# Two heads of q and k share 128 rows in an attention, expert-layer and soft-expert kernel: products and splitting for both heads at once, halves spread by DMA, weight decoding begun two slots later

## The chip, the cores and the metric

One Trainium2 chip, one of its cores. The metric is the device time of one execution in microseconds (us), the median of several runs. The core has five engines with queues of their own: TensorE (PE; its weight loads are listed as PEld), VectorE (DVE), ScalarE (ACT), GpSimd (POOL), and SyncE (SP), which here issues all DMAs.

## The reference, cut to what matters

Three layers run one after the other.

```python
# 1: attention inside clusters; q, k, v are (2, 8, 768, 64), 16 centroids per head
q_assign = argmax(q_n @ c_n.T); k_assign = argmax(k_n @ c_n.T)
mask = q_assign[..., :, None] == k_assign[..., None, :]
scores = where(mask, q @ k.T / sqrt(64), -1e9)
attn = exp(scores - max(scores)); attn /= sum(attn) + 1e-9
x = (attn @ v) laid out as (1536, 512)
# 2: a wide layer with a rational function; w_in and w_out arrive as float64
h = x @ w_in                                   # (1536, 2048)
g = (a0 + a1*h + a2*h**2 + a3*h**3) / (1 + |b0|*|h| + |b1|*h**2 + 1e-6)
x = g @ w_out
# 3: a soft mixture of 8 experts with 4 slots each
logits = x @ phi; slots = softmax(logits, 0).T @ x; each expert: relu(slots @ w1) @ w2
out = softmax(logits, 1) @ expert_outputs
```

## The kernel before

**Slots.** The 16 (batch, head) problems are taken as 8 pairs of heads. A pair has 12 units, one for each of its 2 heads and 6 tiles of 128 query rows, so the attention has 96 slots, numbered `n`; two slots of lead (`LEAD`) come ahead of slot 0. The loop at the end of the attention writes one slot after the other: steps planned for this slot on VectorE and GpSimd (the dictionary `plan`), the transposes of unit n (`turn`, tile `sT`), the exponentials of unit n+1 (`a1_exp`), the copy of `sT` to SBUF (`turned`, tile `eT`), the products of unit n+2 (`a1_mm`, tile `s`), their negated copy with a running minimum on VectorE (`a1_neg`, tile `e`, the row TENSOR_SCALAR_CACHE_REDUCE), planned TensorE steps, and the products with v (`a2_av`, tile `av`). PE, ACT, DVE and POOL keep the order in which the code stands; SP's order is made by a scheduler. `s` and `sT` take turns in two PSUM buffers, so a new `s` waits until the `e` before it has been read, and a new `sT` until the `eT` before it has been copied.

**Preparing a pair.** `prep(p)` returns steps as (offset, kind, function); they are planned four slots into pair p-2 and so spread over the slots behind. They are: products with centroids (`scores`), scaling, transposing (`scT`), argmax (`best`, `first`), a one-hot matrix `oT` and a mask matrix `W`; the part that marks rows of other clusters (`nonhot`, `signed`); and the operands. An fp32 product is made of rounded parts: with a value's rounded high part and the rest as its low part, `q1` holds 64 rows of high and 64 rows of low part, `k1` holds the high part of k twice, and `k2` the low part, with `q2` the high part of q again. A query whose cluster holds no key is zeroed: `alive` is a product that gives 1 or 0 for each query, `qalive` multiplies q by it and by 1/8.

**How the rows lie.** The host hands q and k over transposed and doubled: rows 0 to 63 and rows 64 to 127 of a tile both hold the same head. So a head's split needs no movement between rows: `ksplit(h)` makes `k1` of 128 rows in one GpSimd instruction and `k2` in a second, `qsplit(h, c)` (c is one of two halves of the columns) makes the high part in 128 rows and the low part in rows 64 to 127, and one DMA copies the high rows to `q2`. All of it is done for each head. The first pair has a path of its own (`first_pair`), which runs ahead of the slots. The plan of the second pair's steps is the list `PREP1`.

**Decoding.** Between these steps the float64 weights are turned into fp32, 32 tiles of 128x512 values (`decode_steps`): `bits` (two VectorE instructions), `expo` (ACT), `mant` and `sign` (VectorE), `value` (GpSimd), and for `w_in` `parts` (two on GpSimd), then DMA to DRAM. The list `DEC` says at which slot each tile begins:

```python
DEC = [3 * i if i < 24 else 72 + 2 * (i - 24) for i in range(2 * NF)]
```

**Idle products.** `idle(n)` issues n products of a zero tile, whose result nobody reads. They stand between the steps ahead of the slots and, at the end of the loop's body, in one slot:

```python
        if n < -1:
            idle(2)
```

Behind the attention come 48 units of the wide layer (`h_mm`, `s1` to `s4`), and then the expert layer. The change touches neither.

Of the kernel before, what the change touches and what calls it, by code (L numbers as in the profile page):

```python
# [30 lines left out]
B_MASK = 128  # L31
B_ADD = 448
B_RANK = 768
B_END = 784


def shape_constants():
# [21 lines left out]
def tile_kernel(ctx, tc, qT, kT, v, cenT, cenP, consts, constsb, ab, w_in, w_out, phi, w1, w2, out, dbg=None):  # L59
# [3 lines left out]
    B, H, _, S = qT.shape  # L63
# [48 lines left out]
    cT = att.tile([64, H, 32], F32, name="cT")  # L112
# [8 lines left out]
    PREP1 = (-1, -1, 0, 0, -2, 1, 2, -2, 2, 3, 4, 4, 5, 4, 5, 5, 5, 6, 7, 6, 6, 7, 8, 6, 7, 8, 8)  # L121
# [4 lines left out]
    Ws = [att.tile([96, 384], BF16, name=f"W{i}") for i in range(2)]  # L126
    oTs = att.tile([96, S], BF16, name="oT")
    for t in Ws:
        POOL.memset(t[0:64, 320:384], 0.0)
        POOL.memset(t[64:96, :], 0.0)  # L130
# [4 lines left out]
    def load(p, names="kq"):  # L135
        b, hp = divmod(p, H // 2)
        r = raws.setdefault(p, {})
        for h in range(2):
            for n in names:
                if (p, n) == (1, "k"):  # L140

                    r[n, h] = dec_p.tile([128, 512, 2], I32, tag="raw64", name="rawk1", bufs=2) \
                        .rearrange("p n t -> p (n t)").bitcast(F32)[:, 0:S]
                else:
                    r[n, h] = raw_p.tile([128, S], F32, tag="raw" + n, name=f"raw{n}{h}", bufs=4 if n == "q" else 2)
                SP.dma_start(r[n, h], (kT if n == "k" else qT)[b, 2 * hp + h])
# [11 lines left out]
    def first_pair(r, o, f):  # L158
# [3 lines left out]
        def nonhot_k(h):  # L162
            m = psS.tile([128, 2, 512], F32, tag="S", name="s1")
            for c in range(2):
                PE.matmul(m[64:80, c, 0:HS], hold["W"][0:64, 288 + 16 * h:304 + 16 * h],
# [3 lines left out]
        def nonhot_q(h, c):  # L169
            m = m_tile()  # L170
            w = slice(c * HS, (c + 1) * HS)
            PE.matmul(m[64:80, 0:HS], hold["W"][0:64, 256 + 16 * h:272 + 16 * h], hold["oT"][0:64, w], start=True, stop=True)
            ACT.copy(o[h]["q2"][64:80, w], m[64:80, 0:HS])

        def q0(h):
            w = slice(0, HS)
            q1, q2 = o[h]["q1"], o[h]["q2"]
            qa = hold.pop(("qa", h, 0))
            ACT.copy(q1[:, w], qa)
            POOL.tensor_scalar(q2[0:64, w], qa[0:64, :], 1.0, 1.0, ALU.mult, ALU.mult)  # L180
            DVE.tensor_tensor(q1[64:128, w], qa[64:128, :], q1[64:128, w].bitcast(F32), ALU.subtract)

        def front():
            f["scores"](0)
            f["scores"](1)
            for h in range(2):
                f["ksplit"](h)
# [15 lines left out]
        def back():  # L203
            f["alive"](0, 0)
# [958 lines left out]
```

## Time and profile before

| | |
|---|---|
| time, median of 3 runs | 580.53 us (579.16 to 581.69) |
| the profiled execution | 581.52 us, span 579.70 us, mean granted TensorE clock 0.983 |
| busy over the span | PE 92%, DVE 77%, ACT 65%, POOL 55% |
| ahead of the first `e` | 22.67 us |
| the 96 slots, first `e` to last `e` | 22.67 to 322.19 us |
| the rest (wide layer and experts) | 257.5 us |
| DMA | 116.74 MB, 201 GB/s over the span |

A share over the whole span mixes stages with different limits. The attention is best read slot by slot: the start of one `e` to the start of the next is one slot. The pattern of preparing and decoding repeats every 12 slots (four tiles at three slots each), and so do the rows; one period stands for five. A granted clock of 1.00 is 2.4 GHz, 0.50 is 1.2 GHz.

### The profile page before, as it was taken

How to read it: one execution, taken by the hardware profiler on the slowest of the kernel's cores; microseconds unless marked ns; L12 is line 12 of the kernel's file. 1: busy time of each engine (PE TensorE's matmuls, PEld its weight loads, DVE VectorE, ACT ScalarE, POOL GpSimd, SP SyncE). 2: the span in 40 equal slices, each digit the busy share in tenths (PEclk: the TensorE clock that was granted, in tenths of full speed). 3: DMA queues.
4: the chain of work that ended last, by engine and by line, in shares of the span. 5: the costliest groups of instructions: out<-in, count | busy, mean ns of one | idle time of the engine just before them, and what ended most of it. 6: DMA issues, size and time to landing. Idle time of an engine off the chain costs nothing.

```text
span 579.7 us, 10119 instructions
## 1 busy us (share of the span) xinstructions
PE 534.8 (92%) x3516; PEld 347.7 (60%) x3516; DVE 443.9 (77%) x817; ACT 379.2 (65%) x693; POOL 317.9 (55%) x350
## 2 busy tenths in 40 slices
PE   8869899899898998989889999999999999988994
PEld 2456556465565565655546677777677767743363
DVE  5776978889888888799895379999979997971133
ACT  1666597777776876857768478887778786750111
POOL 3635848668487586694864365555455554611000
PEclk9967999999999999999999999999999999999998
DMA  8634636555474454434531456766576675389997
GB/s 228 220 133 124 188 105 203 164 179 160 148 213 147 136 180 169 145 128 133 171 147 57 144 196 223 270 251 208 178 288 224 228 258 184 118 327 370 421 418 272
DMA packets 40307, 116.74 MB, mean 201 GB/s; under 512 B 5696, under 2 KB 8064, under 8 KB 35648
## 3 DMA queue, kind: packets, MB, share of 16 engines
q1 hardware_dynamic: 40256, 116.09, 57.6%
q8 instruction: 28, 0.46, 0.3%
q14 instruction: 23, 0.19, 0.1%
HBM read 96.02 MB, written 15.73 MB: 193 GB/s over the span
## 4 chain that ended last, share of the span: by engine, by line
PE 67%; DVE 19%; ACT 6%; issue 3%; POOL 2%; DMA 2%; SPq 0%; DVEq 0%; ACTq 0%; POOLq 0%
PE h L779 8%; PE sT L401 8%; PE h L782 8%; PE h L780 8%; PE av L414 6%; DVE e L386 6%; PE s L377 4%; PE s L378 4%; PE gt L840 3%; DVE ex L532 3%; DVE mh L533 3%; PE pb L1014 2%; PE pb L1085 2%; PE mf L237 2%; PE l L846 2%
## 5 line engine op out<-in xcount | busy, mean ns | idle before, releaser
L390 ACT ACTIVATE e<-e,nv 128x768 f32<-128x768 f32 x96 | 90.1, 938 | 80.9 <-DVE e L386 54.7
L386 DVE TENSOR_SCALAR_CACHE_REDUCE e<-s 128x768 f32<-128x768 f32 x96 | 91.5, 953 | 41.3 <-PE s L378 37.0
L401 PEld LDWEIGHTS sT<-cst,e 128*128 128x128 f32 x576 | 63.2, 144 | 61.3 <-ACT eT L407 30.0
L401 PE MATMUL sT<-cst,e 128*128 128x128 f32 x576 | 86.1, 287 | 9.8 <-DVE e L386 7.9
L377 PE MATMUL s<-k,q 128*128 128x384 f32 x192 | 75.6, 394 | 18.3 <-DVE e L386 13.8
L414 PE MATMUL av<-eT,vt 128*64 128x384 f32 x384 | 82.0, 510 | 0.2
L779 PE MATMUL h<-xh,w 128*128 128x512 f32 x192 | 80.6, 420 | 0.0
L407 ACT COPY eT<-sT 128x768 f32<-128x768 f32 x96 | 76.0, 791 | 2.8 <-PE sT L401 2.6
L780 PE MATMUL h<-xl,w 128*128 128x512 f32 x192 | 75.9, 395 | 0.0
L810 POOL TENSOR_SCALAR q<-u,babs 128x512 f32<-128x512 f32 x47 | 36.3, 772 | 69.1 <-ACT u L808 69.0
L548 POOL TENSOR_TENSOR w<-mh,ex 128x512 f32<-128x512 f32 x32 | 41.4, 1293 | 54.2 <-DVE ex L543 42.3
L378 PE MATMUL s<-k,q 80*128 80x384 f32 x192 | 66.8, 348 | 0.0
L812 POOL TENSOR_TENSOR q<-q,u 128x512 f32<-128x512 f32 x47 | 61.0, 1297 | 3.9
L377 PEld LDWEIGHTS s<-k,q 128*128 128x128 f32 x192 | 37.6, 196 | 25.4 <-DVE e L386 15.4
L782 PE MATMUL h<-xh,w 128*128 128x512 f32 x192 | 52.6, 396 | 0.0
L808 ACT ACTIVATE u<-h 128x512 f32<-128x512 f32 x47 | 27.9, 594 | 29.3 <-PE h L782 29.2
L779 PEld LDWEIGHTS h<-xh,w 128*128 128x128 f32 x192 | 36.2, 188 | 16.1 <-DVE p L827 5.0
L811 DVE TENSOR_TENSOR p<-p,h 128x512 f32<-128x512 f32 x47 | 32.1, 683 | 15.9 <-ACT p L809 15.7
L782 PEld LDWEIGHTS h<-xh,w 128*128 128x128 f32 x192 | 36.2, 189 | 8.8
L780 PEld LDWEIGHTS h<-xl,w 128*128 128x128 f32 x192 | 36.2, 188 | 7.2 <-issue 0.5
L819 ACT ACTIVATE r<-q,epsc 128x512 f32<-128x512 f32 (+1 forms) x49 | 33.8, 689 | 8.2 <-POOL q L812 6.7
L827 DVE SCALAR_TENSOR_TENSOR p<-p,ncoef,r 128x512 f32<-128x512 f32 (+1 forms) x49 | 35.9, 732 | 2.7 <-ACT r L820 1.8
(178 smaller groups left out, 1078.3 us busy)
## 6 DMA issues: line engine op xcount, KB each, us to landing
wt<-w SPq DMA_DIRECT2D x32, 1024.0 KB, 7.9
w<-w_in SPq DMA_DIRECT2D x96, 256.0 KB, 3.2
raw<-w_in SPq DMA_DIRECT2D x16, 512.0 KB, 3.3
raw<-w_out SPq DMA_DIRECT2D x16, 512.0 KB, 4.2
w_in<-w SPq DMA_DIRECT2D x16, 512.0 KB, 3.3
rawk<-kT SPq DMA_DIRECT2D x14, 384.0 KB, 3.5
rawq<-qT SPq DMA_DIRECT2D x14, 384.0 KB, 3.8
w_out<-w SPq DMA_DIRECT2D x16, 256.0 KB, 5.2
```

Of the source, the lines that this page charges most:

```text
L377: PE.matmul(ps[:, c, 0:HS], o["q1"][:, it], o["k1"][:, w], start=True, stop=False)
L378: PE.matmul(ps[:, c, 0:HS], o["q2"][0:80, it], o["k2"][0:80, w], start=False, stop=True)
L386: DVE.tensor_scalar(e, s1s.pop(u)[:, :, 0:HS], -1.0, None, ALU.mult, ALU.min, accum_out=nvs[g][:, rest:rest + 1])
L390: ACT.activation(es[u], es[u], AF.Exp, scale=-1.0, bias=nvs[g][:, rest:rest + 1], accum_out=sums[g][:, rest:rest + 1])
L401: PE.transpose(ps[:, j // 3, j % 3 * 128:(j % 3 + 1) * 128], e[:, j, :], ident)
L407: ACT.copy(dst, eTp.pop(u)[:, :, 0:HS].rearrange("p c (j t) -> p c j t", j=3))
L414: PE.matmul(av[g][64 * h:64 * h + 64, 0:HS], vs[g // 2][:, h, j, :], eTs[g][:, h, j, :], start=(j == 0), stop=(j == 5))
L548: POOL.tensor_tensor(w, hold["mh"].bitcast(F32), hold["ex"].bitcast(F32), ALU.mult)
L779: PE.matmul(h, wh[:, c, :], xh[t][:, c, :], start=(c == 0), stop=False)
L780: PE.matmul(h, wh[:, c, :], xl[t][:, c, :], start=False, stop=False)
L782: PE.matmul(h, wl[:, c, :], xh[t][:, c, :], start=False, stop=(c == NCC - 1))
L812: POOL.tensor_tensor(q, q, u, ALU.mult)
```

## The change

Rows 0 to 63 of a tile now hold a pair's first head and rows 64 to 127 its second; q and k are no longer doubled on the host, and half as many bytes are loaded. One `alive` product, one `qalive` and one split serve both heads. The parts then lie in rows of the wrong place, and DMAs from SBUF to SBUF carry them: six of 64x768 for k and six of 64x768 for q for each pair, where before there were none for k and four of 64x384 for q. `ksplit` stands once, at offset 6, instead of at 5 and 8. In the first pair TensorE, ACT, DVE and POOL still make the first half of q in place. `DEC` begins at slot 2 and goes on every 2.65 slots to slot 84; before it went from 0 in steps of 3 to slot 69 and in steps of 2 from 72 to 86. In slots -1 to 5 three idle products are added at the end of each. The first pair's loads are two DMAs of 128 rows instead of eight of 64.

```diff
-    PREP1 = (-1, -1, 0, 0, -2, 1, 2, -2, 2, 3, 4, 4, 5, 4, 5, 5, 5, 6, 7, 6, 6, 7, 8, 6, 7, 8, 8)
+    PREP1 = (-1, -1, 0, 0, -2, 1, 2, 2, 3, 4, 4, 5, 4, 5, 5, 6, 6, 7, 7, 8)
...
-        for h in range(2):
-            for n in names:
...
-                    r[n, h] = raw_p.tile([128, S], F32, tag="raw" + n, name=f"raw{n}{h}", bufs=4 if n == "q" else 2)
-                SP.dma_start(r[n, h], (kT if n == "k" else qT)[b, 2 * hp + h])
+        for n in names:
+            r[n] = raw_p.tile([128, S], F32, tag="raw" + n, name="raw" + n, bufs=2)
+            SP.dma_start(r[n], (kT if n == "k" else qT)[b, hp])
...
-            DVE.tensor_tensor(q1[64:128, w], qa[64:128, :], q1[64:128, w].bitcast(F32), ALU.subtract)
+            DVE.tensor_tensor(q1[l, w], qa[a, :], q1[a, w].bitcast(F32), ALU.subtract)
...
-        def ksplit(h):
-            k1, k2, rk = o[h]["k1"], o[h]["k2"], r["k", h]
-            POOL.tensor_scalar(k1, rk, 1.0, 1.0, ALU.mult, ALU.mult)
-            POOL.tensor_tensor(k2[0:64, :], rk[0:64, :], k1[0:64, :].bitcast(F32), ALU.subtract)
+        def ksplit():
+            ka, kb = tile_(t_p, "ka", [128, S], F32R), tile_(t_p, "kb", [128, S], F32R)
+            POOL.tensor_scalar(ka, r["k"], 1.0, 1.0, ALU.mult, ALU.mult)
+            POOL.tensor_tensor(kb, r["k"], ka.bitcast(F32), ALU.subtract)
+            for h in range(2):
+                a = slice(64 * h, 64 * h + 64)
+                for dst, src in ((o[h]["k1"][0:64, :], ka), (o[h]["k1"][64:128, :], ka), (o[h]["k2"][0:64, :], kb)):
+                    SP.dma_start(dst.bitcast(F32), src[a, :].bitcast(F32))
...
-            POOL.tensor_scalar(q1[:, w], qa, 1.0, 1.0, ALU.mult, ALU.mult)
-            SP.dma_start(q2[0:64, w].bitcast(F32), q1[0:64, w].bitcast(F32))
-            POOL.tensor_tensor(q1[64:128, w], qa[64:128, :], q1[64:128, w].bitcast(F32), ALU.subtract)
+            qa = hold.pop(("qa", c))
+            POOL.tensor_scalar(qh[:, w], qa, 1.0, 1.0, ALU.mult, ALU.mult)
+            POOL.tensor_tensor(ql[:, w], qa, qh[:, w].bitcast(F32), ALU.subtract)
+            if done:
+                for h in range(2):
+                    a, l = slice(64 * h, 64 * h + 64), slice(64 - 64 * h, 128 - 64 * h)
+                    for dst, src in ((o[h]["q1"][a, done], qh), (o[h]["q1"][l, done], ql), (o[h]["q2"][0:64, done], qh)):
+                        SP.dma_start(dst.bitcast(F32), src[a, done].bitcast(F32))
...
-            (12, "P", lambda: alive(0, 0)),
-            (13, "P", lambda: alive(1, 0)),
-            (14, "P", lambda: alive(0, 1)),
-            (15, "P", lambda: alive(1, 1)),
...
+            (12, "P", lambda: alive(0)),
+            (13, "P", lambda: alive(1)),
+            (13, "D", lambda: qalive(0)),
+            (14, "D", lambda: qalive(1)),
+            (14, "G", lambda: qsplit(0)),
+            (15, "G", lambda: qsplit(1, slice(0, S))),
...
-    DEC = [3 * i if i < 24 else 72 + 2 * (i - 24) for i in range(2 * NF)]
+    DEC = [2 + 53 * i // 20 for i in range(2 * NF)]
...
-        if n < -1:
-            idle(2)
+        if n < 6:
+            idle(2 if n < -1 else 3)
```

GpSimd, in the slots in which the third pair's keys are split (`w` and `w_708` belong to decoded tiles, `x`, `xh`, `xl` to finished attention rows), before:

```order
L548 TENSOR_TENSOR w<-mh,ex 128x512
L246 TENSOR_SCALAR k_0_0_116<-rawk_317 128x768
L247 TENSOR_TENSOR k_0_0_117<-rawk_317,k_0_0_116 64x768
L555 TENSOR_SCALAR w_708<-w 128x512
L556 TENSOR_TENSOR w_708<-w,w_708 128x512
L423 TENSOR_SCALAR s<-ssum 128x6
L548 TENSOR_TENSOR w<-mh,ex 128x512
L246 TENSOR_SCALAR k_0_1_120<-rawk_319 128x768
L247 TENSOR_TENSOR k_0_1_121<-rawk_319,k_0_1_120 64x768
L463 TENSOR_SCALAR xh_70<-x 128x384
```

and of the change:

```order
L537 TENSOR_TENSOR w<-mh,ex 128x512
L239 TENSOR_SCALAR ka<-rawk 128x768
L240 TENSOR_TENSOR kb<-rawk,ka 128x768
L544 TENSOR_SCALAR w_748<-w 128x512
L545 TENSOR_TENSOR w_748<-w,w_748 128x512
L420 TENSOR_SCALAR s<-ssum 128x6
L537 TENSOR_TENSOR w<-mh,ex 128x512
L460 TENSOR_SCALAR xh_70<-x 128x384
```

The second head's two key instructions are gone, and nothing takes their place.

SyncE's queue, where the third pair's q is spread (`rawq`, `rawk` are loads for a later pair, `raw` a tile to decode, `w_out` and `w_in` decoded tiles on their way to DRAM), before:

```order
L550 DMA w_out_144<-w 128x512
L326 DMA q_0_0_115<-q_0_0_114 64x384
L326 DMA q_0_1_119<-q_0_1_118 64x384
L146 DMA rawq_1190<-qT 128x768
L326 DMA q_0_0_115<-q_0_0_114 64x384
L146 DMA rawq_1192<-qT 128x768
L526 DMA raw_1102<-w_in 128x1024
L326 DMA q_0_1_119<-q_0_1_118 64x384
```

and of the change:

```order
L539 DMA w_out_144<-w 128x512
L141 DMA rawq<-qT 128x768
L331 DMA q_0_0_114<-qh 64x768
L331 DMA q_0_0_115<-qh 64x768
L331 DMA q_0_0_114<-ql 64x768
L331 DMA q_0_1_118<-qh 64x768
L331 DMA q_0_1_118<-ql 64x768
L331 DMA q_0_1_119<-qh 64x768
L515 DMA raw_1069<-w_in 128x1024
L546 DMA w_in_143<-w_1116 128x1024
```

The six copies now stand in one row, the first head's three in front, and a decode load and a store wait behind them. Before, GpSimd itself wrote `q1`, and only `q2` hung on a copy.

TensorE, in slot 1 of the attention (`sT` of one unit, `s` of the next, then `sT` again), before:

```order
L401 MATMUL sT<-cst,e 128x128 x6
L377 MATMUL s_421<-k_0_1_120,q_0_1_118 128x384
L378 MATMUL s_421<-k_0_1_121,q_0_1_119 128x384
L377 MATMUL s_421<-k_0_1_120,q_0_1_118 128x384
L378 MATMUL s_421<-k_0_1_121,q_0_1_119 128x384
L401 MATMUL sT<-cst,e 128x128 x6
```

and of the change:

```order
L398 MATMUL sT<-cst,e 128x128 x6
L374 MATMUL s_413<-k_0_1_120,q_0_1_118 128x384
L375 MATMUL s_413<-k_0_1_121,q_0_1_119 128x384
L374 MATMUL s_413<-k_0_1_120,q_0_1_118 128x384
L375 MATMUL s_413<-k_0_1_121,q_0_1_119 128x384
L478 LDWEIGHTS zero
L478 MATMUL rest<-zero 128x512
...
L398 MATMUL sT<-cst,e 128x128 x6
```

Three idle products (two of them left out above) now stand between one unit's `s` and the next `sT`, in the place where TensorE had nothing.

## Rows read from the trace of the kernel before

**Rows 1.** The page: busy time per engine

```profile
PE 534.8 (92%) x3516; PEld 347.7 (60%) x3516; DVE 443.9 (77%) x817; ACT 379.2 (65%) x693; POOL 317.9 (55%) x350
```

**Rows 2.** Windows: length, busy PE, PEld, DVE, ACT, POOL, clock, DMA share, GB/s

```profile
22.67:57.63 34.96, 29.07 (x148) 20.56 (x149) 24.62 (x52) 23.29 (x44) 16.60 (x20) 0.76 0.43 138
66.76:104.27 37.51, 34.42 (x231) 21.49 (x233) 31.67 (x61) 27.88 (x53) 26.70 (x31) 1.00 0.56 167
254.79:293.38 38.59, 34.09 (x217) 21.35 (x219) 35.29 (x63) 26.25 (x51) 26.84 (x29) 1.00 0.53 169
293.38:322.19 28.81, 26.88 (x183) 17.06 (x183) 20.09 (x40) 21.70 (x40) 15.14 (x19) 1.00 0.31 113
```

**Rows 3.** Windows of two microseconds in the opening, same columns

```profile
30.00:32.00 2.00, 1.50 (x4) 0.99 (x4) 1.51 (x4) 1.58 (x3) 0.96 (x1) 0.66 0.73 257
44.00:46.00 2.00, 2.00 (x9) 1.69 (x8) 0.00 (x0) 1.87 (x5) 1.16 (x1) 0.50 0.59 207
```

**Rows 4.** Chain that ended last, ahead of the slots: start, length, what

```profile
11.75 1.91 DVE eq L269
...
14.27 0.56 DVE eq L274
```

**Rows 5.** Timeline ahead of the slots: start, length, engine, instruction, count

```profile
10.46 2.75 PE L481 MATMUL rest<-zero 128*128 128x512 bf16 x12
...
11.63 1.80 POOL L247 TENSOR_TENSOR k<-rawk,k 64x768 fp32r<-64x768 f32 x1
```

**Rows 6.** Timeline of VectorE, four instructions of one period

```profile
171.95 1.12 DVE L532 TENSOR_SCALAR ex<-raw 128x512 int32<-128x512 int32 x1
172.99 1.05 DVE L533 TENSOR_SCALAR mh<-raw 128x512 int32<-128x512 int32 x1
...
174.83 1.10 DVE L269 TENSOR_TENSOR eq<-eq,cb 128x384 bf16<-128x384 bf16 x1
...
181.91 1.58 DVE L532 TENSOR_SCALAR ex<-raw 128x512 int32<-128x512 int32 x1
```

**Rows 7.** Timeline of GpSimd, one instruction of the same period

```profile
181.20 2.01 POOL L247 TENSOR_TENSOR k<-rawk,k 64x768 fp32r<-64x768 f32 x1
```

**Rows 8.** Tile raw: durations in ns as minimum/median/maximum

```profile
L532 DVE TENSOR_SCALAR ex<-raw x32: 409/657/1580, 27.9 to 302.0; 128x512 int32<-128x512 int32 x32
L533 DVE TENSOR_SCALAR mh<-raw x32: 415/1046/1527, 28.3 to 302.3; 128x512 int32<-128x512 int32 x32
L539 DVE SCALAR_TENSOR_TENSOR mh<-raw,mh x32: 642/728/1707, 30.8 to 304.1; 128x512 f32<-128x512 uint32 x32
L543 DVE SCALAR_TENSOR_TENSOR ex<-raw,ex x32: 670/683/1464, 33.4 to 307.7; 128x512 int32<-128x512 int32 x32
```

**Rows 9.** Groups by line and shape: busy us, mean ns | idle before

```profile
L247 POOL TENSOR_TENSOR k<-rawk,k 64x768 fp32r<-64x768 f32 x16 | 31.0, 1936 | 1.3
L327 POOL TENSOR_TENSOR q<-qa,q 64x384 fp32r<-64x384 f32 x30 | 30.8, 1027 | 2.5
L325 POOL TENSOR_SCALAR q<-qa 128x384 fp32r<-128x384 f32 x30 | 17.3, 575 | 8.8 <-DVE qa L318 8.2
L318 DVE SCALAR_TENSOR_TENSOR qa<-rawq,mf 128x384 f32<-128x384 f32 x32 | 17.0, 540 | 0.5 <-PE mf L314 0.5
L246 POOL TENSOR_SCALAR k<-rawk 128x768 fp32r<-128x768 f32 x16 | 14.1, 884 | 8.4 <-DMA rawk<-kT 7.9
L314 PE MATMUL mf<-oT,W 80*128 80x384 bf16 x32 | 10.7, 350 | 0.4 <-DVE W L296 0.4
```

**Rows 10.** DMA issues: KB each, median us to landing

```profile
rawk<-kT SPq DMA_DIRECT2D x14, 384.0 KB, 3.5
...
q<-q SPq DMA_DIRECT2D x30, 96.0 KB, 3.0
```

**Rows 11.** Timelines of SyncE and TensorE where the fifth pair's q is first used

```profile
171.73 0.47 SPq L326 DMA_DIRECT2D q<-q  x1
...
175.05 0.41 PE L377 MATMUL s<-k,q 128*128 128x384 f32 x1 [0.28 <-DVE e L386]
```

More of the change, by code (lines that the diff above doesn't have):

```diff
@@ L125, in tile_kernel @@
             for h in range(2)] for i in range(NBUF)]
-    Ws = [att.tile([96, 384], BF16, name=f"W{i}") for i in range(2)]
+    Ws = [att.tile([96, 256], BF16, name=f"W{i}") for i in range(2)]
     oTs = att.tile([96, S], BF16, name="oT")
     for t in Ws:
-        POOL.memset(t[0:64, 320:384], 0.0)
+        POOL.memset(t[0:64, 192:256], 0.0)
         POOL.memset(t[64:96, :], 0.0)
@@ L185, in front @@
             f["scores"](1)
-            for h in range(2):
-                f["ksplit"](h)
+            f["ksplit"]()
             idle(2)
@@ L203, in back @@
         def back():
-            f["alive"](0, 0)
-            f["alive"](1, 0)
-            f["qalive"](0, 0)
-            f["qalive"](1, 0)
+            f["alive"](0)
+            f["qalive"](0)
             nonhot_k(0)
@@ L214, in back @@
             idle(4)
-        rest = [(0, "P", lambda: (f["alive"](0, 1), f["alive"](1, 1))),
-                (1, "D", lambda: (f["qalive"](0, 1), f["qalive"](1, 1))),
-                (1, "G", lambda: (f["qsplit"](0, 1), f["qsplit"](1, 1))),
+        rest = [(0, "P", lambda: f["alive"](1)),
+                (1, "D", lambda: f["qalive"](1)),
+                (1, "G", lambda: f["qsplit"](1, slice(HS, S))),
                 (1, "P", lambda: (nonhot_q(0, 1), nonhot_q(1, 1)))]
@@ L227, in prep @@
         hold = {}
-        order = [r["q", 0], r["q", 1], r["k", 0], r["k", 1]]
         def tile_(pool, tag, shape, dt):
@@ L235, in scores @@
             m = hold["m", c] = m_tile()
-            for g, t in enumerate(order):
-                PE.matmul(m[32 * g:32 * g + 32, 0:HS], cT[:, 2 * hp + g % 2, :],
-                          t[0:64, c * HS:(c + 1) * HS], start=True, stop=True)
+            for g in range(4):
+                a = slice(64 * (g % 2), 64 * (g % 2) + 64)
+                PE.matmul(m[32 * g:32 * g + 32, 0:HS], cT[a, hp, :], r["qqkk"[g]][a, c * HS:(c + 1) * HS],
+                          start=True, stop=True)
         def scaled(c):
@@ L487, in start @@
         SP.dma_start(cT, cenT)
-        r = raws[0] = {}
-        for half in range(2):
-            w = slice(64 * half, 64 * half + 64)
-            for h in range(2):
-                for n in "qk":
-                    if half == 0:
-                        r[n, h] = raw_p.tile([128, S], F32, tag="raw" + n, name=f"raw{n}{h}", bufs=4 if n == "q" else 2)
-                    SP.dma_start(r[n, h][w, :], (kT if n == "k" else qT)[0, h, w])
-            if half == 0:
-                SP.dma_start(cst, consts)
-                SP.dma_start(cb, constsb.bitcast(BF16))
+        load(0)
+        SP.dma_start(cst, consts)
+        SP.dma_start(cb, constsb.bitcast(BF16))
         load(1, "k")
@@ L1127, in lay_out @@
     return {
-        "qT": twice(inputs["q"]),
-        "kT": twice(inputs["k"]),
+        "qT": pairs(inputs["q"]),
+        "kT": pairs(inputs["k"]),
         "v": v,
```

79 lines of the change are left out of this document (35 added, 44 removed).

## The prediction, made before the changed kernel was run

> **What bounds the kernel now.** I read the busy shares first [rows 1]: TensorE is busy 92% of the span, but this is a mean over stages. So next come the windows, cut at the starts of `e` [rows 2]. One period of 12 slots in the middle of the attention takes 37.51 us; TensorE is busy for 34.42 of it at the full clock, VectorE for 31.67, ScalarE for 27.88, GpSimd for 26.70. No engine fills the period. TensorE idles 3.09 us in it, and that is the most that a period can give without taking work from TensorE. The ten slots of the opening (22.67 to 57.63) take 34.96 us, 3.50 a slot against 3.13 in the period, although TensorE has less to do there: the granted clock is 0.76 on average, it falls within 30 to 32 us and is 0.50, that is 1.2 GHz, at 44 to 46 us, with TensorE busy all the time [rows 3]. The last period with decoding (254.79 to 293.38) takes 38.59 us with VectorE busy for 35.29 of them: there a tile is decoded every two slots.
>
> Then I looked at what VectorE does in the four slots of a period in which TensorE waits. The same instruction of the decoding takes 0.41 us at best and 1.58 at worst, the second 0.42 and 1.53 [rows 8]. One of the longest begins at 181.91 and ends at 183.49 [rows 6]; GpSimd's split of a key tile runs from 181.20 to 183.21 [rows 7]. So the VectorE instruction stands until GpSimd's ends, and then takes its usual time.
>
> The Trainium skill, page SBUF — State Buffer, section SBUF: two separate sides, says that VectorE and GpSimd share one port pair as an exclusive lock, which whoever starts first holds for the whole instruction. By that rule every GpSimd instruction taken out can free VectorE for up to its whole length; this trace agrees at the pair of rows just named, and shows no way to tell how often it happens elsewhere.
>
> **The change part by part.** The sum is made against the profiled execution: 581.52 us, span 579.70, 1.82 outside it. That execution is 1.0 above the median of the runs shown.
>
> 1. Ahead of the first `e`. The chain there holds a VectorE instruction of 1.91 us (L269) [rows 4], while GpSimd runs the first key split, 11.63 to 13.43 [rows 5]. Another one on as many bf16 values, L274, takes 0.56 with GpSimd free. That split waited 7.9 us for the load of rows 64 to 127 of k [rows 9], which stood behind the loads that the scores need. Now one load brings all 128 rows, the split can begin when the scores do, and its two instructions (0.88 and 1.94) are over before L269 stands: 1.35 less. One `qalive` of 0.54 leaves the chain [rows 9], which hides nothing else: 0.5 less. The loads bring as many bytes ahead of the scores as before, so I count 0.1 there. Sum -2.0. It is 0 if the split still meets L269, and -3.5 if the loads also land a microsecond and a half sooner.
>
> 2. The opening. TensorE's 29.07 us busy at a clock of 0.76 [rows 2] are 22.1 at full clock. The 21 idle products cost 0.23 each, 2.75 for 12 back to back [rows 5]: 4.8 more, together 26.9. In the period TensorE is busy 34.42 of 37.51, so a stage at the full clock takes 1.09 times its TensorE work: 29.3 instead of 34.96, if the clock stays. VectorE's work (24.62, less two `qalive`) is shorter than that. I take -5.5. The bounds: +2 if the clock falls as before and half of the idle products stand on the path, -8 if the idle products fill only waits.
>
> 3. The five middle periods, 66.76 to 254.79. Per pair GpSimd loses one key split (0.88 and 1.94) and half of the q splits (two of 0.58 and of 1.03) [rows 9], 6.0 of its 26.70 us; a split of 128 rows is costed like one of 64, since the rows of equal columns are the nearest there are. Four stretched VectorE instructions of one period [rows 6] are 1.12, 1.05, 1.10 and 1.58 us; at their best [rows 8] and at L274's 0.56 [rows 4] they would be 0.41, 0.42, 0.56 and 0.41, so 3.05 us is stretch. About half of the splits' instructions go, so I take half, -1.5. Two `alive` products leave TensorE: 0.35 each by their row, overlapped at both ends, -0.5. Two `qalive` leave VectorE, 1.1 us, mostly in slots in which TensorE sets the pace: nothing. Against that a period decodes 12/2.65 = 4.5 tiles instead of 4. A tile is 2.1 us of VectorE at its four minima and 3.1 at its medians [rows 8], half a tile 1.1 to 1.6, of which I put half on the path: +0.7. Net -1.3 a period, -6.5 in five. Bounds: -3.1 a period (all of TensorE's idle time) and +0.8.
>
> 4. The end of the attention. From 254.79 the two-slot rhythm ends: 4.5 tiles instead of 6 in 12 slots take 1.5 x 3.1 = 4.6 us from VectorE's 35.29, and as much as a splitting from GpSimd. Then TensorE sets the pace as in the other periods, 34.09 less one w_out tile and the `alive` products, some 33 x 1.09 = 35.5: about -3. In the last ten slots (28.81) one tile less is open: -1. Bounds: 0 and -6.
>
> 5. The new DMAs. Behind the splits SyncE issues twelve copies per pair instead of four. No engine needs the time of an issue; what matters is when the last of q lands. Before, the last copy is issued at 171.73 and the first product with it stands at 175.05 [rows 11]. The last q step is now two slots (6.3 us) earlier, so the copies begin some 9.6 us ahead of the product. Three issues at 0.47 and a landing between 3.0 us (96 KB) and 3.5 (384 KB) [rows 10] take 5.0: 4.6 us to spare for the first head, and the second is used a slot later. For k there are ten slots. Only the second pair has two slots instead of three, 6.3 us: 1.3 to spare, if GpSimd is on time. I take +0.5, between 0 and +3.
>
> 6. Loads, the smaller mask instruction, other buffers: no wait on them lies on the path in the middle period, where TensorE and VectorE follow each other; if the cover were gone, the 384 KB loads' 3.5 us would be in sight once in a pair. 0. The wide layer and the experts are not touched: 0.
>
> Sum: -2.0 - 5.5 - 6.5 - 4.0 + 0.5 = -17.5, span 562.2, time **564 us**, against a median of 580.5.
>
> **The rivals.**
>
> B, the clock falls in the opening all the same. For it: it fell while VectorE was busy for whole windows, and three short products a slot don't fill such a wait. Against it: the first decode, which made that wait longer, now begins two slots later. Part 2 then gives +1 instead of -5.5: 570.5.
>
> C, the middle periods stay as long as they are. For it: in most slots TensorE is busy throughout, and denser decoding puts back what the splits gave. Against it: the four stretched rows, 1.05 to 1.58 us. Part 3 is 0: 570.5. With B as well, 577.
>
> D, q lands too late in every pair, the case that ends slower. SyncE works in order; a decode load or a store ahead of the copies waits for VectorE or GpSimd, and the copies wait with it. Before, GpSimd wrote `q1` and only `q2` hung on a copy. It costs nothing up to the 4.6 us to spare; each microsecond beyond it is paid in up to seven pairs. From 7.1 us late (17.5 / 7 beyond) it eats the whole gain; at 8.5 late it is 27 us, so 591. Against it: the order puts the copies of one split in one row, with decode traffic behind them.
>
> The Trainium skill, page DMA: Bandwidth & Descriptors, section Anatomy of one DMA, gives each DMA a fixed cost of about 2 us whatever its size, fitted on GpSimd's queue; by that a copy of 192 KB would land in an estimated 2.5 us. No row here has that size, and the 96 KB of rows 10 already take more.
>
> E, most of TensorE's idle time goes, part 3 at -3.0 a period: 555.
>
> F, no change: the changes cancel, or the stretch has another cause, 580.
>
> **How the numbers follow.** Chances: the forecast 0.50, B 0.15, C 0.12, B with C 0.05, D 0.07, E 0.06, F 0.05. The likeliest alone would lie at 558 to 569. To leave out no more than 2 in 10 the range takes in B, C and both together, and stops above E's 555: **554 to 577**. D and the rest of F lie above it. About 0.5% (2.9 us) is what a measurement here can tell from no change, 577.6 to 583.4. Faster: the forecast, B, C, E, and B with C nearly whole, 0.87. Same: F and a mild D, 0.06. Slower: the rest of D, 0.07.
>
> **What would show it.** First `e` near 20.7 us, and L269 near 0.6 ahead of it. Clock 1.00 in windows from 25 to 60 us, the tenth `e` after the first some 29 to 30 us later. In the middle the period under 37 us, VectorE's L532 and L533 (renumbered) with lower medians, GpSimd near 22 us a period. From the 85th slot no two-slot rhythm. It is wrong if TensorE's `s` waits for DMA at a pair's first unit, if the clock is at 0.50 in the opening, or if VectorE's decoding instructions stretch as before, now behind other GpSimd instructions.

## The result, and the profile after

The changed kernel takes **564.9 us** (median, 563.33 to 565.38), the kernel before 581.11 beside it: ratio 0.972, 95% interval 0.9686 to 0.9754. The forecast was 564 us, within 554 to 577, and most likely faster. The total is right; below it turns out that several terms behind it are not, and that its closeness is luck.

The page of the changed kernel, busy time per engine, to be set beside [rows 1]:

```profile
PE 525.6 (94%) x3518; PEld 343.8 (61%) x3521; DVE 425.5 (76%) x801; ACT 378.4 (67%) x693; POOL 276.8 (49%) x304
```

GpSimd lost 41.1 us of work, VectorE 18.4, TensorE 9.2; the span lost 18.3 (579.7 to 561.4). So what went is more than TensorE's own work, and shares alone don't say where. Cut at the starts of `e` as before (the first `e`, the 10th after it, the 13th, then twelves, the 95th), the two profiled executions read:

| stage | before, us | after, us | difference | forecast |
|---|---|---|---|---|
| ahead of the first `e` | 22.67 | 19.95 | -2.72 | -2.0 |
| slots 0 to 10, the opening | 34.96 | 29.77 | -5.19 | -5.5 |
| slots 10 to 13 | 9.13 | 10.43 | +1.30 | none |
| slots 13 to 73, five periods | 188.03 | 184.02 | -4.01 | -6.5 |
| slots 73 to 85 | 38.59 | 34.29 | -4.30 | -3.0 |
| slots 85 to 95 | 28.81 | 25.84 | -2.97 | -1.0 |
| behind the last `e` | 257.51 | 257.10 | -0.41 | 0 |
| span | 579.7 | 561.4 | -18.3 | -17.5 |

The forecast's sum holds +0.5 for the DMAs, which belongs to no one stage.

Windows of the changed kernel, columns as in [rows 2]: the opening and the first two of the five periods.

```profile
19.95:49.72 29.77, 26.68 (x161) 18.09 (x162) 21.62 (x48) 22.34 (x44) 11.58 (x13) 0.94 0.71 189
60.15:94.77 34.62, 33.78 (x229) 21.31 (x231) 30.05 (x60) 27.68 (x53) 22.07 (x25) 1.00 0.77 229
94.77:132.81 38.04, 33.77 (x233) 21.77 (x230) 31.34 (x62) 28.39 (x54) 22.31 (x24) 1.00 0.76 224
```

The periods were alike before (37.41 to 37.83). Now they are not: 34.62, 38.04, 36.64, 38.07, 36.65. TensorE is as busy in the second (33.77) as in the first (33.78) and idles 4.27 us instead of 0.84. Something in the second period makes it wait, and it isn't the amount of work. The windows of two microseconds in which the clock still falls, in the opening:

```profile
40.00:42.00 2.00, 2.00 (x8) 1.25 (x8) 0.00 (x0) 1.60 (x4) 1.81 (x3) 0.50 0.75 255
42.00:44.00 2.00, 2.00 (x10) 1.66 (x11) 0.28 (x1) 0.80 (x1) 0.94 (x1) 0.68 0.23 43
```

VectorE has the answer on the second period. Its tile `raw`, in ns as minimum/median/maximum, to be set beside [rows 8] (L521 and L522 are the two instructions of `bits`, L532 and L533 before):

```profile
L521 DVE TENSOR_SCALAR ex<-raw x32: 409/421/1427, 27.9 to 280.0; 128x512 int32<-128x512 int32 x32
L522 DVE TENSOR_SCALAR mh<-raw x32: 416/1234/1518, 28.2 to 280.4; 128x512 int32<-128x512 int32 x32
```

The first has its best value as median now, but the second's median **rose** from 1046 to 1234 ns. Timelines of VectorE and GpSimd in the second period (start, length, engine, what):

```profile
107.56 1.27 POOL L537 TENSOR_TENSOR w<-mh,ex 128x512 f32<-128x512 f32 x1 [0.69 <-DVE ex L532]
107.63 0.96 DVE L383 TENSOR_SCALAR_CACHE_REDUCE e<-s 128x768 f32<-128x768 f32 x1 [0.22 <-PE s L375]
...
124.33 0.68 DVE L532 SCALAR_TENSOR_TENSOR ex<-raw,ex 128x512 int32<-128x512 int32 x1
124.93 0.42 DVE L521 TENSOR_SCALAR ex<-raw 128x512 int32<-128x512 int32 x1
125.16 1.33 POOL L537 TENSOR_TENSOR w<-mh,ex 128x512 f32<-128x512 f32 x1 [0.85 <-DMA q<-ql]
125.27 1.51 DVE L522 TENSOR_SCALAR mh<-raw 128x512 int32<-128x512 int32 x1
126.46 1.00 POOL L239 TENSOR_SCALAR ka<-rawk 128x768 fp32r<-128x768 f32 x1
127.55 1.84 POOL L240 TENSOR_TENSOR kb<-rawk,ka 128x768 fp32r<-128x768 f32 x1
127.57 2.03 DVE L266 TENSOR_TENSOR eq<-eq,cb 128x384 bf16<-128x384 bf16 x1
```

At 124.33 the `sign` (L532) of one tile begins, the last step of its decoding on VectorE; it ends at 125.01, and GpSimd's `value` (L537), which needs it, starts at 125.16. (The row puts that wait down to a copy of q; but 0.15 us behind the sign is where `value` starts in sign_last too, further below, where the sign comes elsewhere.) In the same slot VectorE has the `bits` of the next tile behind that sign. The first starts ahead of `value` and takes its usual 0.42; the second starts at 125.27, inside `value`, and takes 1.51 us instead of 0.42. So VectorE lets go the very instruction that then holds it. In the whole attention the `bits` stand behind a sign in one slot eleven times, and in nine of them the second takes 1.48 to 1.51 us; of the other two, one has `value` start only behind it, and in one both start together, where `value` is the longer one (1.57 us instead of 1.27). `value` doesn't hold everything: at 107.63 the copy `e`, which reads PSUM, takes its usual 0.96 under the same instruction. At 127.57 the same happens to the argmax instruction L266 behind the key split.

The Trainium skill, page SBUF — State Buffer, section Who interferes with whom, says that VectorE and GpSimd hold one port pair exclusively, whoever issues first, and that a VectorE instruction with at most one SBUF input outside the two-port modes is not touched. `e`, with 0.96 us, agrees; L522, with 1.51, agrees if it runs in such a mode, which no row names.

### The profile page after: what moved, and what is told of

The parts are those of the page before. It is cut to its first block, busy times and chain, and to the rows that moved or that the text cites. A ratio compares the mean times of both kernels' runs of the same rounds, so it can differ in the third digit from the quotient of the medians.

```text
span 561.4 us, 10080 instructions
## 1 busy us (share of the span) xinstructions
PE 525.6 (94%) x3518; PEld 343.8 (61%) x3521; DVE 425.5 (76%) x801; ACT 378.4 (67%) x693; POOL 276.8 (49%) x304
## 4 chain that ended last, share of the span: by engine, by line
PE 67%; DVE 20%; ACT 7%; issue 3%; DMA 2%; DVEq 0%; ACTq 0%
PE h L768 8%; PE h L771 8%; PE h L769 8%; PE sT L398 7%; DVE e L383 7%; PE av L411 6%; PE s L374 4%; DVE mh L522 4%; PE s L375 4%; PE gt L829 3%; PE pb L1074 3%; PE pb L1003 3%; ACT e L387 2%; PE l L835 2%; PE mf L230 2%
## 5 line engine op out<-in xcount | busy, mean ns | idle before, releaser
L398 PE MATMUL sT<-cst,e 128*128 128x128 f32 x576 | 83.9, 282 | 14.1 <-DVE e L383 6.4
L374 PE MATMUL s<-k,q 128*128 128x384 f32 x192 | 73.8, 384 | 6.1 <-DVE e L383 3.7
L537 POOL TENSOR_TENSOR w<-mh,ex 128x512 f32<-128x512 f32 x32 | 42.4, 1325 | 71.4 <-DVE ex L532 31.1
L375 PE MATMUL s<-k,q 80*128 80x384 f32 x192 | 65.0, 339 | 0.0
```

The lines of the kernel that those rows point to most:

```text
L374: PE.matmul(ps[:, c, 0:HS], o["q1"][:, it], o["k1"][:, w], start=True, stop=False)
L375: PE.matmul(ps[:, c, 0:HS], o["q2"][0:80, it], o["k2"][0:80, w], start=False, stop=True)
L398: PE.transpose(ps[:, j // 3, j % 3 * 128:(j % 3 + 1) * 128], e[:, j, :], ident)
L537: POOL.tensor_tensor(w, hold["mh"].bitcast(F32), hold["ex"].bitcast(F32), ALU.mult)
```

## The experiments

All times are medians beside runs of the kernel before on the same chip (578.5 to 581.1 us), ratios with their 95% interval. The chips of the runs differ, so where two kernels lie close the ratios are the better comparison. "Shared rows" is the change without its new dates and without its added idle products; "dates" are those of `DEC`.

### The change taken apart

**pack_dec**: the changed kernel without the added idle products.

```diff
-        if n < 6:
-            idle(2 if n < -1 else 3)
+        if n < -1:
+            idle(2)
```

> The changed kernel without the 21 added idle products. If the idle products hold the clock in the opening, the ten slots behind the first e go from 29.8 back towards 34 us and the whole to 568 to 570 us (ratio to the kernel before 0.978 to 0.981), with a clock of 0.50 in some windows between 25 and 55 us. Rival: the opening is shorter because the first decode comes later and VectorE has less to do; then the time stays at 564 to 566 us, and the clock is no lower than with them.

563.62 us, ratio 0.972 (0.9671 to 0.9768): the rival's time. The clock did drop (mean 0.88 over the opening, 0.94 with the idle products), as the theory has it and the rival does not, yet the opening took 28.20 us, less than with the idle products (29.77). With them the chain that ended last runs through three of them at 39.95 us, 1.39 us long at the fallen clock: there they stand on the path.

**pack_idle**: the changed kernel with the old dates.

```diff
-    DEC = [2 + 53 * i // 20 for i in range(2 * NF)]
+    DEC = [3 * i if i < 24 else 72 + 2 * (i - 24) for i in range(2 * NF)]
```

> The changed kernel with the decoding list of before (steps of 3, then of 2, from slot 0). If the even pace gave the end of the attention, the last 22 slots grow by about 5 to 7 us, the five middle periods shrink by 2 to 4 us (half a tile less each), and the whole is 567 to 570 us. Rival: the shared rows alone shortened the end, since the splits of the last pairs are halved; then the whole stays at 564 to 566 us.

558.05 us, ratio 0.9623 (0.9576 to 0.967). Neither answer expected that: the old dates are **faster** than the new ones by 1%. The first of the five periods, window as above:

```profile
56.61:91.71 35.10, 33.75 (x229) 21.25 (x231) 28.35 (x59) 27.79 (x53) 20.99 (x25) 1.00 0.73 206
```

All five lie at 35.02 to 35.42, 2.4 under those of before. Slot by slot the difference is mostly one slot: 4.49 us before, 2.81 here. Before, the second head's key split ran there, and two VectorE instructions stretched under it (the first of the five periods; [rows 6] and [rows 7] hold the same slot of the fourth):

```profile
67.65 1.08 DVE L274 TENSOR_TENSOR eq<-eq,mr 128x384 bf16<-128x384 bf16 x1
68.41 1.99 POOL L247 TENSOR_TENSOR k<-rawk,k 64x768 fp32r<-64x768 f32 x1
...
69.12 1.57 DVE L532 TENSOR_SCALAR ex<-raw 128x512 int32<-128x512 int32 x1
```

Now VectorE reads (L271 is L274 of before, L521 is L532):

```profile
57.49 0.56 DVE L271 TENSOR_TENSOR eq<-eq,mr 128x384 bf16<-128x384 bf16 x1
...
58.43 0.42 DVE L521 TENSOR_SCALAR ex<-raw 128x512 int32<-128x512 int32 x1
```

**dec_idle**: the kernel before with the new dates and the idle products, no shared rows.

```diff
-    DEC = [3 * i if i < 24 else 72 + 2 * (i - 24) for i in range(2 * NF)]
+    DEC = [2 + 53 * i // 20 for i in range(2 * NF)]
...
-        if n < -1:
-            idle(2)
+        if n < 6:
+            idle(2 if n < -1 else 3)
```

> The kernel before with the new decoding list and the added idle products, without shared rows. If the parts add up as in the forecast, opening and end come (about -5 and -4), the middle grows by 2 to 4 us, and the start stays: 573 to 576 us. Rival: only the shared rows matter, 579 to 582 us.

587.36 us, ratio 1.0127 (1.0087 to 1.0167): 1.3% slower than before, which neither answer expected. The opening fell to 29.49 and the last ten slots to 26.08, but the middle periods rose to as much as 42.31.

**pack**: shared rows alone, old dates, no added idle products (both edits above on the changed kernel).

> Shared rows alone: the old dates of decoding and no added idle products. Theory from the run without them under the new dates: the idle products change nothing that can be told, 557 to 560, and the ten slots of the opening stay near 28 us although the clock drops for some microseconds. Rival: with the old dates the first decode stands in slot 0, TensorE waits for it without idle products, the clock falls to half in the opening and the ten slots take 30 to 32 us: 561 to 563.

555.82 us, ratio 0.9609 (0.9554 to 0.9664), just under the theory's range. The whole gain and more is in the shared rows. The opening and two windows in it:

```profile
19.77:47.70 27.93, 23.18 (x145) 16.62 (x144) 21.65 (x49) 22.99 (x45) 11.79 (x14) 0.94 0.70 198
...
28.00:30.00 2.00, 1.84 (x8) 1.88 (x9) 1.08 (x4) 1.62 (x4) 0.84 (x1) 0.51 0.93 184
30.00:32.00 2.00, 2.00 (x12) 1.54 (x11) 1.02 (x3) 0.50 (x1) 1.83 (x3) 0.64 0.81 269
```

The clock falls to half here for some microseconds, and the opening is 7.0 us shorter than before all the same. It falls for less long, though: its mean over the opening is 0.94, against 0.76 before, without one idle product added.

**idle**: the kernel before with the 21 idle products alone.

```diff
-        if n < -1:
-            idle(2)
+        if n < 6:
+            idle(2 if n < -1 else 3)
```

> The kernel before with the 21 idle products alone. Theory: as in the other pair of kernels they are worth nothing, because they lie in waits of TensorE or in front of work that VectorE limits: 579 to 582, the ten slots of the opening at 34 to 36 us. Rival, the prediction's own: they hold the clock, which was 0.76 over the ten slots, and the opening takes 29.5 us: 574.5 to 576.

577.63 us, ratio 0.9965 (0.9941 to 0.9989). The time lies between the two answers, the stage is the rival's. The window of the opening shows what the prediction said, clock 1.00 and 29.93 instead of 34.96:

```profile
22.78:52.71 29.93, 26.24 (x167) 17.73 (x170) 25.22 (x52) 23.09 (x44) 16.76 (x20) 1.00 0.49 161
```

The profiled span is 4.1 us under that of before, the median 2.9 (2.0 by the ratio). So idle products mend the opening, and shared rows mend it too, but not twice: with both it is 27.81.

### Is it the second key split?

**twice_k**: the changed kernel with a second key split per pair that nobody reads, at offset 9, near where the second head's split stood.

```diff
-    PREP1 = (-1, -1, 0, 0, -2, 1, 2, 2, 3, 4, 4, 5, 4, 5, 5, 6, 6, 7, 7, 8)
+    PREP1 = (-1, -1, 0, 0, -2, 1, 2, 2, 3, 3, 4, 4, 5, 4, 5, 5, 6, 6, 7, 7, 8)
...
+        def again():
+            kc = hold["sc"].bitcast(F32R)
+            POOL.tensor_scalar(kc, r["k"], 1.0, 1.0, ALU.mult, ALU.mult)
+            POOL.tensor_tensor(kc, r["k"], kc.bitcast(F32), ALU.subtract)
...
+            (9, "G", again),
```

> The changed kernel with a second key split for each pair but the first, three steps after the first one and written to a tile that nobody reads: about 2.8 us more of GpSimd per pair, as before the change. If GpSimd's splits stretch VectorE's decoding on the path, 1.5 us in each of seven periods, the whole goes to 572 to 576 us. Rival: GpSimd's time is off the path, and the time stays within 1 us of 564.9.

566.81 us, ratio 0.9767 (0.9711 to 0.9823), an overlap with the changed kernel's interval, so that the 2 us are not clear of none. In the first of the five periods the copy costs what the theory says (36.21 us against 34.62): L527 (L521 of the changed kernel) takes 1.58 us under it, L276 (L271) 1.07. In the others it stretches VectorE instructions as well, but in three of the four a slot behind gives back part of what the copy takes, or more than all (in the second period +0.75 and then -1.53 us); the fourth grows by 2.29, at a fallen clock (see below). Why a slot behind gets shorter, no run shows. The theory had been read from the old dates, so the same copy went under those.

**twice_k_pack_idle**: the same addition to pack_idle.

> Shared rows and idle products with the old dates of decoding (558.05 us), and a second key split per pair at offset 9 that nobody reads, where the second head's split of the kernel before stood. Theory: the gain of the middle periods is that this split no longer meets VectorE's decoding and argmax instructions in one slot; put back, it makes that slot 4.5 us again instead of 2.8, +1.7 us in each of seven pairs, and the time 568 to 572. Rival: GpSimd has room and VectorE's stretch has another cause, so that the copy costs what it cost in the changed kernel, about 2 us in all: 559 to 561.

569.93 us, ratio 0.9837 (0.9797 to 0.9876): 12 us more than without the copy, as the theory said. The slot is 4.44 us again, and its timeline shows who waits for whom (L248 and L249 are the copy):

```profile
57.83 0.82 POOL L248 TENSOR_SCALAR sc<-rawk 128x768 fp32r<-128x768 f32 x1
58.05 1.02 DVE L276 TENSOR_TENSOR eq<-eq,mr 128x384 bf16<-128x384 bf16 x1
58.74 2.00 POOL L249 TENSOR_TENSOR sc<-rawk,sc 128x768 fp32r<-128x768 f32 x1
...
59.46 1.57 DVE L527 TENSOR_SCALAR ex<-raw 128x512 int32<-128x512 int32 x1
```

L276 takes 1.02 instead of 0.56, L527 1.57 instead of 0.42, together 1.61; the period is 36.73 instead of 35.10, 1.63 more. The other periods grow by 1.61 to 1.65 as well. So one instruction pair of GpSimd costs by its place, not by its length of 2.8 us: 12 us under the old dates, about 2 under the new.

### What the new dates cost

**sign_last**: the changed kernel with one digit changed. D2 steps stand behind D1 steps in a slot, so the `bits` of the next tile come ahead of the `sign`.

```diff
-        return [(-3, "S", dma), (0, "D1", bits), (1, "A", expo), (1, "D1", mant), (2, "D1", sign),
+        return [(-3, "S", dma), (0, "D1", bits), (1, "A", expo), (1, "D1", mant), (2, "D2", sign),
```

> The changed kernel with one step moved: where the sign of one weight tile and the bits of the next fall in one slot, the sign comes behind the bits on VectorE instead of ahead of them; the dates of the tiles stay. Theory: the new pace costs because GpSimd's product of mantissa and exponent (1.3 us) starts the moment the sign ends and holds VectorE's next bits, 1.43 to 1.5 us instead of 0.42. With the sign behind the bits that stretch goes in one or two of the five slots with two tiles in a period: each period some 1 us shorter than 34.6 to 38.1, the middle median of the second of the bits well under 1.0 us, and the time 559 to 561. Rival: the pace costs for another reason (more VectorE work in a period), and the stretch only moves to the mantissa or the sign: 563 to 566, as the changed kernel.

**553.1 us**, ratio 0.9544 (0.9504 to 0.9583), 11.8 under the changed kernel (10 by the ratios) and more than expected. The tile `raw`, and the same slot of the second period as above:

```profile
L522 DVE TENSOR_SCALAR mh<-raw x32: 412/429/1512, 28.0 to 270.3; 128x512 int32<-128x512 int32 x32
```

```profile
120.29 0.42 DVE L521 TENSOR_SCALAR ex<-raw 128x512 int32<-128x512 int32 x1
120.62 0.42 DVE L522 TENSOR_SCALAR mh<-raw 128x512 int32<-128x512 int32 x1
120.96 0.68 DVE L532 SCALAR_TENSOR_TENSOR ex<-raw,ex 128x512 int32<-128x512 int32 x1
121.56 0.95 DVE L383 TENSOR_SCALAR_CACHE_REDUCE e<-s 128x768 f32<-128x768 f32 x1
121.79 1.27 POOL L537 TENSOR_TENSOR w<-mh,ex 128x512 f32<-128x512 f32 x1 [1.53 <-DMA q<-ql]
```

The median of L522 falls from 1234 to 429 ns. `value` now starts when VectorE goes on to `e`, which it doesn't touch, and L522 keeps its 0.42. The instructions behind `e` are still held a little (L266 takes 0.84 us here, 2.03 in the changed kernel, 0.36 at its best); this slot and the next together take 5.68 us instead of 7.35.

**no_pack_sign_last**: the same edit on dec_idle.

> The kernel before with the new dates and the idle products, each head still split by itself, and the sign behind the next tile's bits. The same without the moved sign took 587.36 us. Theory: the new dates lose because the sign lets GpSimd start where the bits of the next tile stand; with the sign behind them the middle periods fall from 37.4 to 42.3 us to about 37, and with the opening at 29.5 and the end at 26 the time is 565 to 572, under the kernel before. Rival: the second key split is what the new dates collide with, so the periods stay near 41 and the time at 582 to 588.

579.29 us, ratio 1.0017 (0.9987 to 1.0046), between the two answers: the moved sign gives back 8 us of dec_idle (6 by the ratios), but two middle periods stay at 41.59 and 43.33. In them the splits of the single heads still meet the decoding; in the second of the two:

```profile
181.01 1.81 POOL L247 TENSOR_TENSOR k<-rawk,k 64x768 fp32r<-64x768 f32 x1
181.14 1.97 DVE L532 TENSOR_SCALAR ex<-raw 128x512 int32<-128x512 int32 x1
```

**sign_last_no_idle**: sign_last without the added idle products, the edit of pack_dec.

> The changed kernel with the sign behind the bits (553.1 us), without the 21 added idle products. Theory: with shared rows the idle products are worth nothing in the opening, as in the two pairs of kernels before it: 551.5 to 554.5. Rival: here GpSimd and VectorE leave TensorE waiting less, but the first decode begins two slots later and there is less ahead of it; without idle products the clock drops to half, and the ten slots of the opening grow from 27.1 to 29 us or more: 555 to 557.

554.46 us, ratio 0.9569 (0.9514 to 0.9624), as the theory has it; the opening takes 26.75 us at a mean clock of 0.94, with them 27.08 at 1.00.

**sign_last_old_dates**: sign_last with the old dates, the edit of pack_idle.

> Shared rows and idle products with the old dates (558.05 us), the sign behind the next tile's bits. With the old dates two tiles meet in one slot only behind slot 72. Theory: the 12 slots from 73 to 85 fall from 35.5 to about 33.5 us and the ten behind them by up to 1, all others stay at 35.0 to 35.4: 554.5 to 556. Rival: at two slots a tile VectorE itself is the limit there, and the end stays at 35.5 and 27.8: 557.5 to 559.

555.87 us, ratio 0.9593 (0.9538 to 0.9648). The time is in the theory's range, but the stage refutes it: slots 73 to 85 took 36.50 us, not 33.5 (pack_idle: 35.52). At two slots a tile the stretch has given way to a wait for the next load, in a slot of 5.13 us:

```profile
265.98 0.43 DVE L521 TENSOR_SCALAR ex<-raw 128x512 int32<-128x512 int32 x1 [2.88 <-DMA raw<-w_out]
```

There are two buffers for `raw`, and `sign` is the last to read one. The timeline points to that later place as what delays the load: the sign ends at 260.19, stretched to 1.50 us, and the load is issued at 260.22; in pack_idle they stand at 258.30 and 258.72, and the wait for the load is 1.07. No run tried it by itself.

**sign_last_k9**: sign_last with the key split at offset 9.

```diff
-            (6, "G", ksplit),
+            (9, "G", ksplit),
```

> The changed kernel with the sign behind the bits, and the key split at offset 9 instead of 6. Theory: GpSimd has room in either place and the new dates put other tiles there in every period, so it costs in some periods what it saves in others: 551 to 555, as without the move. Rival: at offset 9 it holds the argmax and mask instructions of VectorE that all of a pair's preparation waits for, as the copy did under the old dates, +1.6 us a period: 561 to 565.

557.71 us, ratio 0.9627 (0.9561 to 0.9692), between the answers: some 5 us lost. The profile shows one meeting of the moved split with a decode, in the first of the five periods (37.43 us against sign_last's 34.95):

```profile
92.11 1.88 POOL L240 TENSOR_TENSOR kb<-rawk,ka 128x768 fp32r<-128x768 f32 x1
92.22 2.04 DVE L522 TENSOR_SCALAR mh<-raw 128x512 int32<-128x512 int32 x1
```

All kernels beside each other; the stages are those of the table above, from each one's profiled execution, whose own time and mean granted clock over slots 13 to 73 stand beside them:

| kernel | time, us | ratio | profiled, us | slots 0 to 10 | 13 to 73 | clock there | 73 to 95 |
|---|---|---|---|---|---|---|---|
| changed | 564.9 | 0.972 | 563.33 | 29.77 | 184.02 | 1.00 | 60.13 |
| pack_dec | 563.62 | 0.972 | 567.91 | 28.20 | 186.80 | 0.98 | 59.77 |
| pack_idle | 558.05 | 0.9623 | 556.31 | 27.81 | 176.05 | 1.00 | 63.36 |
| pack | 555.82 | 0.9609 | 555.14 | 27.93 | 176.09 | 1.00 | 63.38 |
| idle | 577.63 | 0.9965 | 577.35 | 29.93 | 187.99 | 1.00 | 67.44 |
| dec_idle | 587.36 | 1.0127 | 586.9 | 29.49 | 200.51 | 0.97 | 63.47 |
| no_pack_sign_last | 579.29 | 1.0017 | 578.94 | 28.48 | 197.31 | 0.96 | 61.36 |
| sign_last | 553.1 | 0.9544 | 552.84 | 27.08 | 179.89 | 1.00 | 58.35 |
| sign_last_no_idle | 554.46 | 0.9569 | 555.19 | 26.75 | 177.59 | 1.00 | 58.35 |
| sign_last_old_dates | 555.87 | 0.9593 | 556.52 | 27.78 | 176.07 | 1.00 | 64.20 |
| sign_last_k9 | 557.71 | 0.9627 | 562.12 | 27.08 | 185.59 | 0.98 | 58.91 |
| twice_k | 566.81 | 0.9767 | 568.22 | 28.56 | 187.55 | 0.98 | 60.71 |
| twice_k_pack_idle | 569.93 | 0.9837 | 570.65 | 28.43 | 184.19 | 1.00 | 67.09 |

The stages come from one execution each; in pack_dec and sign_last_k9 it took 4.3 and 4.4 us more than the median. Where the clock column is under 1.00 the clock is at or near its lowest in slots 49 to 61: they took 40.69 us at a mean of 0.95 in pack_dec, 40.36 at 0.92 in twice_k, 39.95 at 0.91 in sign_last_k9, 42.31 at 0.92 in dec_idle and 43.33 at 0.88 in no_pack_sign_last, against 38.07 at 1.00 in the changed kernel and 35.64 at 1.00 in sign_last. In no_pack_sign_last the clock falls behind two microseconds (183 to 185) in which TensorE was not busy at all. So in these five kernels, all with the new dates, a part of the longest periods is likely the clock's; how much was not separated.

The new dates are a trade. Against pack_idle, sign_last loses 3.84 us in the five periods and gains 5.01 in the end.

## Why the prediction was right in the total and wrong in parts

**1, ahead of the first `e`** (forecast -2.0, measured -2.72): right in its mechanism, L266 takes 0.36 where L269 took 1.91 [rows 4]. A second meeting, which the sum doesn't name, went with it. Before, the last VectorE instruction ahead of the first `e` stood under a key split of the second pair; now it (L177) takes 0.62 us:

```profile
20.21 2.01 POOL L247 TENSOR_TENSOR k<-rawk,k 64x768 fp32r<-64x768 f32 x1
20.68 1.95 DVE L181 TENSOR_TENSOR q<-qa,q 64x384 fp32r<-64x384 f32 x1 [0.15 <-ACT q L179]
```

A part was given back. The chain now ends in products with centroids for the second pair, 1.42 us from 17.58, and the first `s` stands behind them. And the prediction didn't look at the norms of the centroids: the split now starts at 5.57, and VectorE is just then at work on those norms, four columns wide (timelines of the changed kernel):

```profile
5.57 0.84 POOL L239 TENSOR_SCALAR ka<-rawk 128x768 fp32r<-128x768 f32 x1 [3.00 <-DMA rawk<-kT]
5.64 0.77 DVE L500 SCALAR_TENSOR_TENSOR pc<-pc 128x4 f32<-128x4 f32 x1
6.49 1.81 POOL L240 TENSOR_TENSOR kb<-rawk,ka 128x768 fp32r<-128x768 f32 x1
...
6.64 1.69 DVE L502 TENSOR_SCALAR pc<-pc 128x4 f32<-128x4 f32 x1
...
11.30 0.36 DVE L266 TENSOR_TENSOR eq<-eq,cb 128x384 bf16<-128x384 bf16 x1
```

Both VectorE instructions end with GpSimd's, at 6.41 and at 8.3; the same line L500 takes 0.16 us at 5.04, ahead of the split. The chain runs through them to the scaling of the scores at 8.64, which began at 8.80 before: the earlier load brought only 0.16 there.

**2, the opening** (-5.5; -5.19): the size was right, the reason only in part. The step "if the clock stays" took idle products as its condition. They do hold the clock in the kernel before (idle: 29.93 us at 1.00, near the 29.3 of the sum). But shared rows alone bring the mean clock from 0.76 to 0.94, and with them the opening is short with added idle products (pack_idle, 27.81 at 1.00) or without (pack, 27.93 at 0.94). So the likely reading, not shown apart, is that shared rows shorten the waits behind which the clock fell; what is left of its fall costs nothing that can be told. In the changed kernel itself the clock fell to 0.50 in spite of the idle products, as rival B had it, without B's price. With the idle products the new dates cost 2.0 us of the opening (29.77 against 27.81), without them 0.3 (28.20 against 27.93); in slots 10 to 13 they cost 1.3 and 2.1 more, which the prediction did not see.

**3, the five periods** (-6.5; -4.01): two terms mis-sized in opposite senses, and one of them by a missing mechanism. Shared rows give -2.4 a period (pack_idle), against -2.0 for the prediction's -1.5 and -0.5. (The prediction held that the trace can't tell how often a split meets VectorE; the two timelines beside each other, as above, tell it.) The slot of the second key split alone gives -1.68; the two slots with `alive` give 0.34 (3.26 and 3.25 to 3.09 and 3.08). "Denser decoding, +0.7" measured +1.6: 184.02 less 176.05, over five. It was priced as VectorE work for half a tile. About half of it, 0.8, goes when the sign moves behind the bits (sign_last, 179.89), so that half was the order of sign, value and bits. What stays beside the old dates is 0.8 with the idle products and 0.3 without (sign_last_no_idle 177.59, pack 176.09), of the size that was priced. The step that failed is the one that prices a tile by its number in a period: it did not ask which instructions the new distances bring into one slot.

**4, the end of the attention** (-4; -7.27): mis-sized and put down to the wrong cause. With the two-slot rhythm kept, shared rows already bring slots 73 to 85 from 38.59 to 35.52; ending the rhythm adds 1.23, not 3 (1.20 in the kernel before: 38.59 to 37.39 in dec_idle). In the last ten slots shared rows give 0.97 and the new dates 2.0; the last tile then begins two slots sooner.

**5, the DMAs** (+0.5; no wait of TensorE on them): right in the result by a narrow margin, with a wrong landing. DMA issues of the changed kernel (columns as in [rows 10]), then SyncE and TensorE where the fifth pair's q is first used, beside [rows 11]:

```profile
k<-ka SPq DMA_DIRECT2D x32, 192.0 KB, 6.3
q<-qh SPq DMA_DIRECT2D x28, 192.0 KB, 5.9
rawk<-kT SPq DMA_DIRECT2D x8, 384.0 KB, 6.8
...
q<-ql SPq DMA_DIRECT2D x14, 192.0 KB, 6.0
```

```profile
156.84 1.15 SPq L331 DMA_DIRECT2D q<-qh  x2
158.08 0.55 SPq L331 DMA_DIRECT2D q<-ql  x1
...
164.97 0.42 PE L374 MATMUL s<-k,q 128*128 128x384 f32 x1
```

The landing was taken as 3.0 to 3.5 us from rows of a kernel with fewer transfers; it is 5.9 to 6.0. The third copy of the first head, issued at 158.08, lands by this median at about 164.1, 0.9 us ahead of the product, where the prediction had 4.6 to spare. In two of the kernels a first product does wait for these copies, 0.6 us in sign_last_no_idle and 1.1 in sign_last_k9. Rival D was nearer than its chance says.

**6** (0; -0.41 behind the last `e`): nothing to explain.

Of the signs named in advance, the first `e`, the tenth `e` (29.77), and the missing two-slot rhythm came out; the period under 37 us in three of five; the lower median of the second decoding instruction did not, nor did the clock of 1.00 (0.50 from 40 to 42 us). Both were named as what would make the prediction wrong: a clock at 0.50 in the opening, and decoding instructions that stretch as before behind other GpSimd instructions. The total came out because terms 3 and 4 missed by +2.5 and -3.3, and slots 10 to 13, which had no term, by +1.3. That is luck.

**Open.** Under the new dates the five periods differ even where the clock stays at 1.00: 34.62 to 38.07 us in the changed kernel, against 35.02 to 35.42 with the old dates (pack_idle). Why the new dates are so sensitive was not tried; nor what the fallen clock costs by itself in the middle periods, nor a start of the first pair's split behind the norms.

## What to carry to other kernels

An instruction on GpSimd can cost by the VectorE instructions that it meets and by what stands behind them, so its place is to be costed, not its length: the same copied split cost 12 us under one order and about 2 under another. Where VectorE produces what releases GpSimd, put that step last among a slot's VectorE steps, ahead of one that reads PSUM; under the new dates this alone took 11.8 us off, under the old dates, where two tiles meet in a slot only behind slot 72, about 2 (558.05 to 555.87). Take a changed kernel's DMA landings from its own coming traffic, not from that of the kernel before, and test parts of a change apart: beside the shared rows the two other parts here were worth nothing or less, while the sum looked right.

## What the hardware showed that was not expected

A VectorE instruction on four columns, 0.16 us long, lasts 0.77 and another of that width 1.69 us when a GpSimd split of 768 columns has begun; both end with it. The median landing of a 384 KB load of k rose from 3.5 to 6.8 us as the span's mean traffic went from 201 to 224 GB/s; the copies between SBUF rows alone are not the cause, for in twice_k_pack_idle, with the same copies, it is 3.3. And with shared rows TensorE at 1.2 GHz for some microseconds cost nothing measurable in the opening (27.93 us at a mean of 0.94, 27.81 at 1.00), while in the kernel before holding the clock took it from 34.96 at 0.76 to 29.93.
